# Gate logits from the transposed x on TensorE, or from a second copy of x on VectorE

## The chip, the core and the metric

The kernel runs on one core of a Trainium2 chip. Its engines each work through their own queue in order: TensorE (PE, matrix products; its weight loads are listed as PEld), VectorE (DVE), ScalarE (ACT), GpSimd (POOL) and SyncE (SP, which here only starts DMA transfers). The metric is the device time of one execution in microseconds (us), as the median of several runs.

## The reference

Two attention blocks read the same x of 2048 rows and 1024 columns in bf16, and a gate mixes them row by row. Block A is linear attention over 32 heads of width 32, block B looks at 8 earlier positions, two apart.

```python
x = A_x
g = _sigmoid((x * gate_w).sum(-1, keepdims=True))
a = _A_ref(x, A_wqkv, A_wo)     # phi(q) (phi(k)^T v) / (phi(q) sum(phi(k))), then @ wo
b = _B_ref(x, B_wqkv, B_wo)     # softmax over 8 positions, dilation 2, then @ wo
return g * a + (1 - g) * b      # phi(t) = where(t > 0, t + 1, exp(t)) + 1e-6
```

The gate needs one logit for each of the 2048 rows. With l the logit, the result is (exp(l) * a + b) / (1 + exp(l)); the kernel keeps exp(l) in the tile nel and 1 / (1 + exp(l)) in the tile omg, both 128 x 16: a column for each of the 16 tiles of 128 rows.

## The kernel before, in words

x is read as even and odd rows (two parities, 8 tiles of 128 rows each) and lies transposed in xT, so that it can be the operand of every projection. Two row tiles make a pair; there are 8 pairs.

Most products go by a scheme with seven block products in place of eight (class Group). A group multiplies a 2 x 2 block of x with a 2 x 2 block of weights. Its products m1 to m7 are four matmuls of 512 columns each, and accumulate in the PSUM banks X and Y, of which there are two of each, used by groups in turn. ScalarE saves partial results (M1s, U2s, U4s, line 273), VectorE adds them to the other partial results (acc, line 246). Sums of x blocks (xsums, lines 100 to 103) and of weight blocks (sums, lines 131 to 134) are prepared by VectorE. run (line 427) writes the order of PE by hand: m1 and m2 of the new group, m3 of the one before, m6, m4 of the one before, m7, m5. A bank of Y is thus written by m2, read by VectorE, written again by m7 of the same group, read, added to by m4, read, and then given to the group after the next.

The queues of PE and SP have exactly the order in which the program issues their instructions. The other engines' order is made by a scheduler that keeps dependences and goes by priority. After every product, side (line 384) counts one step on, takes at most one of the deferred VectorE tasks (dve_side, line 405) and, when its turn has come, one step of side work. defer(n, ops, gap) puts a list of VectorE tasks n products ahead; each is placed behind the last accumulation that has been issued (issue_after). later(n, f) calls f n products on. The first due list of deferred tasks goes first; the others wait for the next product.

The stages, in the time of the profile: values of block B (vb_plain and vb_group, lines 505 to 546) to about 70 us, mixed from 48 us on with keys and queries of B (k_group, q_group); then, to about 290 us, a round of four groups that returns every 29.4 us: keys of A for a pair (ka_group), keys of B, values of A (va_group) and queries of B. In that round the attention of B runs as side work: scores into s (line 702, one tile of four PSUM banks, also used for kps, o and oA), their exponentials PT on ScalarE (line 707), masked by VectorE (line 708), the products o with vw (lines 718 and 723), nB and oB on VectorE (lines 730, 734, 736) and a store to OB_d (line 738). The kps matmuls (line 585) take the keys' features eA (phi, line 549: an Exp on ScalarE and three VectorE tasks, lines 552 to 554) and the values vA of a pair. From 290 us follow the queries of A (qa_plain, qa_group, qa_out) and the output projection (out_group).

The gate logits before: gate(t) issues 8 matmuls, one for each 128 of the 1024 columns, with a 128 x 128 tile of xT as weights and one column of gw as the moving operand, into one column of gps (line 456). vb_plain calls it for the first four tiles, the main program for the others, before the groups of pairs 2 to 5. gate_end (line 459) makes nel and omg with two Exp on ScalarE and two VectorE operations. gw is loaded by POOL (line 181). nel is first read by POOL at line 631, in qa_out; omg scales the output groups.

## Time and profile before

| What | us |
|---|---|
| median of 3 runs | 460.13 (459.77 to 460.38) |
| the profiled execution | 459.77 |
| its span | 458.0 |
| TensorE busy in it | 442.6 |
| VectorE busy in it | 283.3 |
| ScalarE busy in it | 237.2 |
| GpSimd busy in it | 60.1 |

The span begins with the first instruction of the profile and ends with the last; what lies around it belongs to the run's time. A row of a timeline or of a chain gives the start, the length, the engine, the source line and the operation with the tile that it writes and the tiles that it reads. The lengths of successive operations of one engine overlap a little, so that the distance from start to start is shorter than the length. Where a row ends in square brackets, they hold the engine's idle time before it and what ended it. In a row of a window the numbers are its time, then the busy time of PE, PEld, DVE, ACT and POOL with their instruction counts, the granted clock of TensorE as a share of full speed (1.00 throughout this profile), the busy share of the DMA engines and what they moved in GB/s.

### The profile page before, as it was taken

To read this page: it belongs to the slowest core of one execution; us is meant where nothing else is said; L and a number is where in the kernel's file an instruction comes from. 1 tells how busy PE (TensorE), PEld (TensorE's weight loads), DVE (VectorE), ACT (ScalarE), POOL (GpSimd) and SP (SyncE) were. 2 spreads that over 40 slices of the span, in tenths; PEclk is the share of its full clock that TensorE was granted. 3 is DMA by queue.
4 is the path that set the end of the run, shared out by engine and by line. 5 is a ranking of instruction groups with operands and counts; after the bars stand their busy time and mean duration, and the time that the engine had idled before them with its cause. 6 is when DMAs were issued, how large, how long until landed. Compare 5 with 4: busy or idle time off the path is not lost.

```text
span 458.0 us, 11713 instructions
## 1 busy us (share of the span) xinstructions
PE 442.6 (97%) x5017; PEld 216.6 (47%) x5070; DVE 283.3 (62%) x452; ACT 237.2 (52%) x345; POOL 60.1 (13%) x119
## 2 busy tenths in 40 slices
PE   8999999998999999999999999999999999999996
PEld 5454444444444444444444444445554444444444
DVE  0566668679657486484774846669777982256112
ACT  3233457467476474673846838536676544222221
POOL 8100000000000000000000000008686314000000
PEclk9999999999999999999999999999999999999999
DMA  8899801880302603007030076291229772795111
GB/s 213 194 203 269 277 2 72 239 158 26 76 4 61 132 3 99 1 27 165 5 99 3 24 156 192 77 253 47 71 79 217 164 173 92 155 204 135 48 46 47
DMA packets 111956, 51.62 MB, mean 113 GB/s; under 512 B 75552, under 2 KB 107552, under 8 KB 111904
## 3 DMA queue, kind: packets, MB, share of 16 engines
q1 hardware_dynamic: 111600, 50.61, 45.9%
q8 instruction: 39, 0.64, 0.6%
q10 hardware_dynamic: 272, 0.26, 0.2%
q14 instruction: 13, 0.11, 0.1%
q0 software_dynamic: 32, 0.00, 0.0%
HBM read 26.22 MB, written 16.78 MB: 94 GB/s over the span
## 4 chain that ended last, share of the span: by engine, by line
PE 90%; ACT 7%; issue 1%; DVE 0%; ACTq 0%; DVEq 0%
PE X L264 41%; PE Y L264 28%; PE Q L667 9%; PE K L520 3%; ACT PT L707 3%; PE o L718 2%; PE oA L624 2%; ACT eA L551 2%; PE s L702 1%; PE kps L585 1%; ACT tA L244 1%; PE o L723 1%; PE Y L299 1%; ACT U2s L273 1%; PE gps L467 1%
## 5 line engine op out<-in xcount | busy, mean ns | idle before, releaser
L264 PEld LDWEIGHTS <-xT 128*128 128x128 bf16 (+1 forms) x352 | 33.0, 98 | 39.6 <-issue 1.8
L264 PE MATMUL X<-T,SS 128*128 128x512 f16 x176 | 45.3, 380 | 0.7 <-ACT U2s L273 0.7
L264 PEld LDWEIGHTS <-WS 128*128 128x128 bf16 (+1 forms) x288 | 28.1, 98 | 33.6
L667 PE MATMUL Q<-xT,WS 128*128 128x512 bf16 x186 | 43.1, 379 | 0.3
L264 PE MATMUL X<-SS,TS 128*128 128x512 f16 x144 | 37.0, 379 | 4.0 <-ACT U2s L273 3.9
L273 ACT COPY U4s<-X 128x512 f32<-128x512 f32 x40 | 23.4, 585 | 33.2 <-PE X L264 33.1
L486 POOL MEMSET vA<- 128x32 bf16 x16 | 4.0, 250 | 268.0 <-DVE eA L554 144.8
L264 PE MATMUL Y<-W,xT 128*128 128x512 bf16 (+1 forms) x152 | 39.0, 379 | 0.0
L264 PEld LDWEIGHTS <-SS 128*128 128x128 f16 x264 | 24.3, 98 | 29.7 <-issue 2.8
L707 ACT ACTIVATE PT<-s 128x2048 bf16<-128x2048 f32 x16 | 29.9, 1870 | 15.1 <-PE s L702 15.0
L264 PE MATMUL Y<-xT,WS 128*128 128x512 bf16 (+1 forms) x144 | 37.0, 379 | 0.0
L264 PEld LDWEIGHTS <-TS 128*128 128x128 f16 x216 | 20.5, 98 | 29.0 <-issue 5.9
L708 DVE TENSOR_TENSOR PT<-PT,maskp 128x2048 bf16<-128x2048 bf16 x16 | 19.6, 1224 | 22.1 <-ACT PT L707 22.1
L273 ACT COPY M1s<-X 128x512 f32<-128x512 f32 x40 | 23.6, 591 | 11.5 <-PE X L264 10.4
L667 PEld LDWEIGHTS <-WS 128*128 128x128 bf16 x192 | 18.3, 98 | 20.1
L273 ACT COPY U2s<-X 128x512 f32<-128x512 f32 x40 | 23.4, 584 | 8.2 <-PE X L264 8.2
L264 PEld LDWEIGHTS <-oT 128*128 128x128 bf16 (+1 forms) x176 | 17.1, 98 | 20.8 <-DMA oT<-OA_d 0.5
L635 POOL TENSOR_TENSOR obA<-ofv,rec 128x512 bf16<-128x512 f32 x22 | 25.6, 1184 | 0.9
L730 DVE COPY nB<-o 128x1024 f32<-128x1024 f32 x16 | 19.5, 1222 | 6.2 <-ACT rB L729 6.2
L729 ACT ACTIVATE rB<-o 128x1024 f32<-128x1024 f32 x16 | 16.4, 1025 | 12.4 <-DVE oB L736 8.2
L264 PE MATMUL X<-T,oS 128*128 128x512 f16 x96 | 22.7, 379 | 0.0
L264 PE MATMUL X<-W,SS 128*128 128x512 bf16 x86 | 22.5, 379 | 0.1
(140 smaller groups left out, 760.1 us busy)
## 6 DMA issues: line engine op xcount, KB each, us to landing
V_d<-va SPq DMA_DIRECT2D x16, 256.0 KB, 3.2
WS<-in_B_wqkv_dram SPq DMA_DIRECT2D x16, 256.0 KB, 4.2
W<-in_A_wqkv_dram SPq DMA_DIRECT2D x8, 512.0 KB, 5.9
vw<-V_d SPq DMA_DIRECT2D x16, 256.0 KB, 4.4
OB_d<-oB SPq DMA_DIRECT2D x16, 256.0 KB, 2.2
OA_d<-obA SPq DMA_DIRECT2D x16, 256.0 KB, 2.3
out_dram<-osb SPq DMA_DIRECT2D x30, 128.0 KB, 1.8
oT<-OB_d SPq DMA_DIRECT2D x12, 256.0 KB, 4.0
```

Of the source, the lines that this page charges most:

```text
L264: nc.tensor.matmul(ps[:], lhsT=lhsT, rhs=rhs, start=start and kc == 0, stop=kc == self.nk - 1, skip_group_check=True)
L273: nc.scalar.copy(out=s[:], in_=ps[:])
L520: nc.tensor.matmul(ps[:], lhsT=xT[p][:, kc, i, c * P:c * P + P], rhs=wvB.W[:, kc, 512 * j:512 * j + 512], start=kc == 0, stop=kc == 7, ski ...
L551: return [lambda: (nc.scalar.activation(out=e, in_=t, func=ACT.Exp), nc.vector.tensor_scalar(out=t, in0=t, scalar1=0.0, scalar2=None, op0= ...
L624: nc.tensor.matmul(o[:, k, 132 * j:132 * j + 132], lhsT=es[i][:, j, k * P:(k + 1) * P], rhs=KVz[:, nn + 4 * j, :], start=True, stop=True)
L635: nc.gpsimd.tensor_tensor(out=ob[:, k:k + 2], in0=of[:, k:k + 2, :, 0:32], in1=rec[:, k:k + 2].broadcast_to([P, 2, 8, 32]), op=ALU.mult)
L667: nc.tensor.matmul(ps[:], lhsT=w.W[:, kc, j * P:j * P + P], rhs=xT[p][:, kc, i, :], start=kc == 0, stop=kc == 7, skip_group_check=True)
L707: nc.scalar.activation(out=PT[:], in_=s[:], func=ACT.Exp, scale=SCALE)
L708: nc.vector.tensor_tensor(out=PT[:], in0=PT[:], in1=maskp[:, None, :].broadcast_to([P, 4, 512]), op=ALU.mult)
L718: nc.tensor.matmul(o[32 * g:32 * g + 32, 2 * b, cols], lhsT=vw[rows, j, 4 * ch + g, :], rhs=PT[rows, g, cols], start=True, stop=True)
L729: nc.scalar.activation(out=rB[:], in_=o[:, 1:4:2, :], func=ACT.Ln)
L730: nc.vector.tensor_copy(out=nB[:], in_=o[:, 0:4:2, :])
```

## The change

The gate matmuls, gw's load by POOL and all calls of gate in the early stage are taken out. From the stage of B's keys and queries on, gates() loads the gate row into the first half of a new tile gx, in all 128 partitions alike, and 44 products later calls gate(0). gate(t) loads the 128 rows of tile t, as they are in x, into the second half of gx. Four products later VectorE gets two tasks, one product apart: each multiplies 512 columns with the gate row, in place, and puts the sums over the columns into logit. With the second task the next tile's gate is called, so its load is issued then; it overwrites the same half of gx. After tile 15, gate_end adds the two halves and makes nel (one Exp) and omg from nel. gx has the buffer that is later used by the tile of of qa_out; an assertion there says that nel has been issued.

In the lists of the other engines the following moves: some of the VectorE tasks of phi come a product later, because the pieces have taken their turn, and one of x's sums comes earlier in the first stage. PE keeps its order apart from the matmuls that are left out.

```diff
-    gw = consts.tile([P, 8], BF16, name="gw")
-    nc.gpsimd.dma_start(out=gw[:], in_=gate_w.rearrange("(k p) -> p k", p=P))
...
-    gps = gps_tile[:, 0, 0:16]
+    gx = ofp.tile([P, 2, D], BF16, name="gx", tag="of", bufs=1)
+    logit = consts.tile([P, 2, 16], F32, name="logit")
 
     def gate(t):
-        p, j = divmod(t, 8)
-        hf, c = divmod(j, 4)
-        for kc in range(8):
-            nc.tensor.matmul(gps[:, t:t + 1], lhsT=xT[p][:, kc, hf, c * P:(c + 1) * P], rhs=gw[:, kc:kc + 1],
-                             start=kc == 0, stop=kc == 7)
+        gw, xg = gx[:, 0, :], gx[:, 1, :]
+        nc.sync.dma_start(out=xg, in_=xrows(t))
+
+        def part(h):
+            cols = slice(512 * h, 512 * h + 512)
+            nc.vector.scalar_tensor_tensor(out=xg[:, cols], in0=xg[:, cols], scalar=1.0, in1=gw[:, cols],
+                                           op0=ALU.mult, op1=ALU.mult, accum_out=logit[:, h, t:t + 1])
+            if h:
+                gate(t + 1) if t < 15 else gate_end()
+        defer(4, [lambda: part(0), lambda: part(1)])
 
     def gate_end():
-        nc.scalar.activation(out=nel[:], in_=gps, func=ACT.Exp)
-        nc.scalar.activation(out=omg[:], in_=gps, func=ACT.Exp)
-        nc.vector.tensor_scalar(out=omg[:], in0=omg[:], scalar1=1.0, scalar2=None, op0=ALU.add)
+        ready.add("nel")
+        nc.vector.tensor_tensor(out=nel[:], in0=logit[:, 0, :], in1=logit[:, 1, :], op=ALU.add)
+        nc.scalar.activation(out=nel[:], in_=nel[:], func=ACT.Exp)
+        nc.vector.tensor_scalar(out=omg[:], in0=nel[:], scalar1=1.0, scalar2=None, op0=ALU.add)
         nc.vector.reciprocal(out=omg[:], in_=omg[:])
+
+    def gates():
+        nc.sync.dma_start(out=gx[:, 0, :], in_=bass.AP(gate_w.tensor, gate_w.offset, [[0, P], [1, D]]))
+        later(44, lambda: gate(0))
...
-            gate(tile_of(*t))
             v_final(vs[t[0]], True)(t[1], 0, ps[t][:], None)
...
+            assert "nel" in ready
...
-    gates(2)
...
-    later(2, lambda: gates(3))
...
-    gates(4, 5)
...
-    gates(6, 7)
-    gate_end()
...
+    gates()
     run(lambda: vb_group(6), RATE_R)
```

## The prediction

> **What bounds the kernel now.** I read the page first: TensorE is busy in nearly every slice, VectorE is not.

> ```profile
> PE 442.6 (97%) x5017; PEld 216.6 (47%) x5070; DVE 283.3 (62%) x452; ACT 237.2 (52%) x345; POOL 60.1 (13%) x119
> PE   8999999998999999999999999999999999999996
> DVE  0566668679657486484774846669777982256112
> ```

> So a microsecond taken from TensorE (PE) is a microsecond of time, and work on VectorE (DVE) is free as long as PE never waits for it. Next, the chain that ended last, in order of time, and the view of line 456, the gate matmuls that go:

> ```profile
> 32.70 0.78 PE gps L456 x32
> 39.55 0.78 PE gps L456 x32
> ...
> L456 PE MATMUL gps<-gw,xT x128: 163/163/167, 10.0 to 40.2; 128*128 128x1 bf16 x128
> ```

> All gate work lies on that chain before 41 us: 32 matmuls push the next product back by 0.78 us, 24 ns each; the 163 ns of one overlap. Then the stretch in which the new VectorE work falls, as a window (time, PE, PEld, DVE, ACT, POOL, clock, DMA), and its timeline at the places where PE follows VectorE closely:

> ```profile
> 112.70:207.00 94.30, 91.35 (x1457) 44.16 (x1469) 63.63 (x102) 59.82 (x78) 1.68 (x7) 1.00 0.22 54
> ...
> 118.91 0.69 DVE L246 TENSOR_TENSOR qT<-Y,M1s 128x512 bf16<-128x512 f32 x1
> 119.75 1.03 PE L264 MATMUL Y<-xT,WS 128*128 128x512 f16 x4
> 119.95 0.69 DVE L246 TENSOR_TENSOR vA<-Y,U2s 128x512 bf16<-128x512 f32 x1 [0.36 <-PE Y L264]
> 121.57 0.68 PE L585 MATMUL kps<-vA,eA 128*32 128x33 bf16 x64
> ...
> 139.14 1.22 DVE L730 COPY nB<-o 128x1024 f32<-128x1024 f32 x1
> 140.41 0.74 PE L718 MATMUL o<-PT,vw 64*32 64x57 bf16 x72
> ...
> 156.08 0.69 DVE L246 TENSOR_TENSOR qT<-Y,U2s 128x512 bf16<-128x512 f32 x1 [1.54 <-PE Y L264]
> 156.84 0.77 PE L702 MATMUL s<-qT,kT 32*64 32x57 bf16 x72
> ```

> The reader is to see four thin slacks, from VectorE's end to the PE start that depends on it: qT from M1s frees the Y bank of the next product, 0.15 us; vA from U2s is read by the kps matmuls, 0.93; the copy nB frees o for the second o matmuls, 0.05; qT from U2s is read by the scores, 0.07. The places recur every 29.4 us; the slack of the first varies from 0.15 to 1.6, the last two stay under 0.4. Last, prices of loads and of the nearest VectorE operation:

> ```profile
> OB_d<-oB SPq DMA_DIRECT2D x16, 256.0 KB, 2.2
> xr<-in_A_x_dram SPq DMA_DIRECT2D x2, 256.0 KB, 3.6
> out_dram<-osb SPq DMA_DIRECT2D x4, 64.0 KB, 1.6
> ...
> 299.69 1.28 DVE L677 SCALAR_TENSOR_TENSOR eq<-Q,eq 128x512 bf16<-128x512 f32 x2
> ```

> **What is removed.** 128 gate matmuls with their weight loads. The chain's pieces add to 0.38+0.18+0.18+0.38+0.38+0.78+0.78 = 3.1 us. This shortens the time in full: PE's longest idle before 42 us that is not start-up is 0.5 us behind a ScalarE copy, and that copy moves up with PE. The transposed x loads are the nearest cover to fail: SP issues them 1.5 us apart from 22.76, so those of pair 4 (the first two, 5.7 us to landing) are in by 30; the group that reads them moves from 33.3 to 31.0. Also gone are POOL's gate load (1.04 us, on an engine busy 13% of the span), one Exp of 0.18 on ScalarE, and two small VectorE operations moved to about 207: nothing. POOL now clears maskp (0.54) ahead of ident's select; the transposes wait for xr, landing 3.9, and ident is ready near 2: nothing.

> **What is added.** One broadcast load of the gate row, 60 us before use: nothing. Sixteen loads of 256 KB on SP and 32 pieces on VectorE; a piece is a 512-column scalar_tensor_tensor with an accumulator output. The pieces of tile t must finish before SP may load tile t+1 into the same buffer, and the program issues the first piece of t+1 four products later. By the changed program's instruction order, tile 0's pieces stand before the copy nB at 114.10 and tile 15's after L736 at 204.93.

> *Price of a piece:* two L677 take 1.28, one 0.68, so one follows the other by 0.60. For the accumulator I add 0.06, half the 0.12 between the tiny VectorE operation at 41.14 and its successor. Ends: 0.33 (the pace of the 512-column 16-bit sums, 33.97 to 34.30) and 0.92 (the slower scalar_tensor_tensor of L855, 0.75, with a whole tiny operation of 0.17). I take 0.66, as L677 is the same operation and width.

> *Price of a load:* stores of 64 and 256 KB land after 1.6 and 2.2, 0.003 us per KB; the quickest vw load lands after 2.1, taken as one of 32 KB; 224 KB more make 2.8. Ends: 2.0 (quickest OB_d store) and 4.1 (slower xr load, among other loads). I take 2.8.

> *What it does.* 32 x 0.66 = 21 us fit the 30.7 us that VectorE idles in the stretch. But VectorE works in order: a first piece whose load hasn't landed stops every accumulation queued behind it. I walked the changed order through this profile's times, before's clock throughout, each operation at its start-to-start pace; D is how far PE has fallen back.
> - Tile 0 and the exponentials' operations that the pieces push behind them: qT from M1s ends at 120.24 and the product due at 119.75 starts at 120.3: 0.55. Tile 1's load stands on SP behind both OB_d stores, whose second waits for L736 (117.4): issued 117.75, landed 120.55. Its pieces run 120.75 to 122.07, ahead of vA from U2s, so kps, due 122.12, starts 122.8: 0.7. D 1.25.
> - Tile 3's second piece ends 133.86, tile 4's load lands 136.7, VectorE stands idle for it 1.6 us; the work behind makes nB end at 142.87, and the second o matmuls, due 141.66, start 142.95: 1.3. D 2.55.
> - Tile 6 puts tA from M1s to 158.64, product due 158.43: 0.3. Its second piece ends 156.92, tile 7's load lands 159.75, both pieces stand ahead of qT from U2s, which ends 161.76; scores due 159.64: 2.2. D 5.0.
> - Tiles 8 to 10, same way: qT from M1s 0.8. D 5.85.
> - Tile 12's first piece waits for its load until 192.05; scores due 192.08, start 193.45: 1.4. D 7.2.
> - Tiles 14 and 15: nB 0.2, the product on Y before vA's U4s is read 0.3. D 7.7.

> ScalarE's new nel waits for tile 15 ahead of the copies vA and U2s; U2s ends at 216.1, its reader is due at 216.5: nothing. nel is first used by POOL's rec near 300. SP's queue: the WS load of 154.35 now stands behind tile 8's load until 161.1, its sums stood at 165.87 and D moves them to 170.9: nothing. vw is delayed by 2 to 3 us, read 17 us later: nothing. Should those covers go, the price is the delay itself.

> Sum: 7.7 - 3.1 = +4.6 us. The profiled execution took 459.77 us (span 458.0 and 1.77 around it), the median of the three runs is 460.13, 0.36 above; so 464.4 by the profile and **464.7** as a median. With both prices at their low ends D is about 0.6 (net -2.5, 457.6), with both high about 20 (net +17, 477).

> [...]

> **Rivals.**
> - *The cover holds (faster).* VectorE has the idle time, and four products of 0.86 us, 3.5 us, lie between a tile's last piece and the next one's first. If pieces take 0.42 and loads 2.2, the walk leaves D at about 1.9: net -1.2, 458.9. It decides where D passes 3.1: with loads at 2.2 that is a piece of about 0.55. Against it: the tiles' pieces stand directly ahead of qT from U2s, and L677's pace.
> - *Loads are slow here.* WS loads in this stretch took 4.6 (146.80 to the sums at 151.44) and share the queue. At 4.1 and 0.66 each of four waits grows by 1.3, and two more (tile 2's, tile 11's) by about 1: D 15, net +12, 472.
> - *The gates cost nothing where they were* (the start bound by loads): the 3.1 is not gained, 467.8. Against: PE stands in the chain throughout.
> - *Mere occupancy:* the loads hide and only the pieces push: of the terms 0.55, 0.7, 0.3, 0.8, 0.2 and 0.3 stay, 2.9, against 3.1: 459.9.

> **How the numbers follow.** Forecast (+1 to +9) 0.60; slow loads or a dear accumulator (over +9) 0.10; gates free 0.03; mere occupancy, within 0.2% (0.92 us, about what this kernel's measurement can tell) 0.10; cover holds 0.17. Slower is 0.73. The range leaves out a tenth below and a tenth above: 458.9, the cover case, to 471, near the slow loads. The forecast's own range is 461 to 469.

> **What would show it.** Before 41 us: no L456, and everything after it about 3.1 us early until 112. Then in 112 to 220: 32 pieces near 0.7 each, VectorE waiting for gx loads ahead of qT from U2s, PE waits at scores, kps and o put down to VectorE, DVE busy over 85%. After about 220 the two profiles should run in step, some 4.6 us apart. Wrong if gx loads land within about 2.2 us or pieces take 0.4: then PE shows no new waits.

## The result, and the profile after

The changed kernel takes 464.93 us (median, 464.78 to 467.14), the kernel before 460.10 beside it (459.77 to 460.38): a ratio of 1.0116, with a 95% interval of 1.0085 to 1.0147. It is slower by 4.8 us; the forecast was 464.7. The profiled execution took 465.0, its span is 463.2 against 458.0.

From the page of the changed kernel: busy times, then busy tenths of PE and DVE and the granted clock in 40 slices of 11.6 us.

```profile
PE 441.7 (95%) x4890; PEld 213.5 (46%) x4942; DVE 302.1 (65%) x517; ACT 236.8 (51%) x344; POOL 59.0 (13%) x118
...
PE   8999999999988899999999999999999999999996
...
DVE  0576777679678698697683755759777883256112
...
PEclk9999999999998999999999999999999999999999
```

PE is busy for 0.9 us less in a longer span: the three 8s, from 127 to 162 us, are new. One slice, from 139 us, also has a lower clock; the kernel before has a 9 in all forty.

The view of the tile gx (durations in ns: least, median, most; then idle time by what ended it; then the loads' trip):

```profile
L457 DVE SCALAR_TENSOR_TENSOR gx<-gx x32: 680/686/694, 110.1 to 210.7; 128x512 bf16<-128x512 bf16 x32
L457 DVE DVE_READ_ACCUMULATOR gx<-gx x32: 80/83/89, 110.7 to 211.3; 128x1 f32 x32
...
  DMA gx<-in_A_x_dram: 10.3, 5
...
DMA to landing us min/median/max: 2.6/2.8/6.1
```

VectorE stood idle 10.3 us in five waits for these loads. The chain of waits around the most expensive one, followed back from 145 us (start, us, what):

```profile
124.81 2.80 DMA gx<-in_A_x_dram
...
127.70 0.70 DVE gx L457 x2
...
130.14 0.62 DVE gx L457 x2
...
130.78 3.38 DMA gx<-in_A_x_dram
...
134.25 0.70 DVE gx L457 x2
134.95 0.60 DVE tA L244
135.55 1.13 DVE PT L717
136.68 0.61 DVE gx L457 x2
...
139.17 1.15 DVE nB L739
140.31 0.04 issue
140.35 0.74 PE o L727 x72
```

In this view, `DVE gx L457 x2` is one piece with the read of its accumulator. So the rows are tile 3's load, its two pieces, tile 4's load, its first piece, two operations that stand between in VectorE's order, its second piece, and behind that everything up to the copy nB, which the second o matmuls wait for. The waits of PE (us, times, longest) name all places of the forecast but that of tile 6:

```profile
PE o L727 <- DVE nB L739: 2.8, 3, 2.0
PE s L711 <- DVE qT L244: 2.3, 2, 1.3
...
PE Y L262 <- DVE qT L244: 0.7, 2, 0.5
...
PE kps L593 <- DVE vA L244: 0.4, 1, 0.4
```

And the clock, in windows around the wait for nB (time, PE busy, clock, DMA share, GB/s):

```profile
137.59:141.00 3.41, 1.39 (x84) 1.00 0.22 77
141.00:144.41 3.41, 3.19 (x26) 0.50 0.21 82
```

For 3.41 us from 141.00 PE runs at half clock. The table lists by how much each place pushed PE back, from the starts of the same matmuls in the two profiles; the changed kernel comes to 110 us with a lead of 2.95.

| place (start before, after) | forecast | measured |
|---|---|---|
| product behind qT, tile 0 (119.75, 117.19) | 0.55 | 0.40 |
| product behind kps, tile 1 (122.18, 120.07) | 0.7 | 0.45 |
| second o matmuls, tile 4 (140.41, 140.35) | 1.3 | 2.06 |
| half clock (143.08, 144.66) | none | 1.64 |
| tA from M1s, tile 6 | 0.3 | 0 |
| product behind the scores, tile 7 (157.53, 160.46) | 2.2 | 1.35 |
| tiles 8 to 10 (178.52, 182.11) | 0.8 | 0.67 |
| scores, tile 12 (186.93, 191.60) | 1.4 | 1.08 |
| tiles 14, 15 (207.08, 212.09) | 0.5 | 0.34 |
| D | 7.7 | 7.99 |

The distance between the profiles is 5.0 us from there on (score matmuls start at 274.48 and 279.49), and with the lead of 2.95 that makes 7.96; the rows add to 7.99 because each is rounded.

### The profile page after: what moved, and what is told of

Read it like the earlier page. It is cut to its first block, busy times and chain, and to the rows that moved or that the text cites. A ratio compares the mean times of both kernels' runs of the same rounds, so it can differ in the third digit from the quotient of the medians.

```text
span 463.2 us, 11566 instructions
## 1 busy us (share of the span) xinstructions
PE 441.7 (95%) x4890; PEld 213.5 (46%) x4942; DVE 302.1 (65%) x517; ACT 236.8 (51%) x344; POOL 59.0 (13%) x118
## 4 chain that ended last, share of the span: by engine, by line
PE 74%; DVE 9%; ACT 6%; DMA 5%; issue 2%; SPq 2%; DVEq 0%; ACTq 0%
PE X L262 33%; PE Y L262 23%; PE Q L676 9%; DMA gx<-in_A_x_dram 4%; PE K L529 3%; DVE gx L457 3%; ACT PT L716 2%; PE o L727 2%; PE oA L633 1%; DVE nB L739 1%; ACT eA L559 1%; SPq L816 1%; DMA oT<-OA_d 1%; PE s L711 1%; ACT tA L242 1%
## 5 line engine op out<-in xcount | busy, mean ns | idle before, releaser
L262 PEld LDWEIGHTS <-xT 128*128 128x128 bf16 (+1 forms) x352 | 33.3, 98 | 40.7 <-issue 2.6
L457 DVE SCALAR_TENSOR_TENSOR gx<-gx 128x512 bf16<-128x512 bf16 x32 | 21.2, 687 | 10.4 <-DMA gx<-in_A_x_dram 10.3
## 6 DMA issues: line engine op xcount, KB each, us to landing
V_d<-va SPq DMA_DIRECT2D x16, 256.0 KB, 3.3
WS<-in_B_wqkv_dram SPq DMA_DIRECT2D x16, 256.0 KB, 4.8
vw<-V_d SPq DMA_DIRECT2D x16, 256.0 KB, 5.1
OB_d<-oB SPq DMA_DIRECT2D x16, 256.0 KB, 2.2
gx<-in_A_x_dram SPq DMA_DIRECT2D x16, 256.0 KB, 2.8
OA_d<-obA SPq DMA_DIRECT2D x16, 256.0 KB, 2.3
```

Source lines behind the costliest of these rows:

```text
L262: nc.tensor.matmul(ps[:], lhsT=lhsT, rhs=rhs, start=start and kc == 0, stop=kc == self.nk - 1, skip_group_check=True)
L457: nc.vector.scalar_tensor_tensor(out=xg[:, cols], in0=xg[:, cols], scalar=1.0, in1=gw[:, cols], op0=ALU.mult, op1=ALU.mult, accum_out=logi ...
```

## The experiments

The theory: a piece costs little; what costs is that the next load is issued only when the second piece has read the buffer, so that its trip stands in VectorE's order ahead of accumulations that PE waits for. Rivals: the pieces' own 20 us on an engine that is nearly the bound, and, for the half clock, a cause other than the wait. D is always PE's place against the kernel's own place before 110 us, measured at the score, o and kps matmuls.

### No pieces at all

```diff
 def gates():
-    nc.sync.dma_start(out=gx[:, 0, :], in_=bass.AP(gate_w.tensor, gate_w.offset, [[0, P], [1, D]]))
-    later(44, lambda: gate(0))
+    nc.vector.memset(logit[:], 0.0)
+    later(44, gate_end)
```

> The changed kernel without the sixteen x loads, the gate row load and the 32 pieces: logit is cleared once, so the gate is 1/2 everywhere and the logits are not computed. It measures what taking the gate matmuls off TensorE is worth by itself. Theory (the gates stood on the chain, 3.0 us of it): about 457.1 us, 3.0 under the kernel before. Rival (the early stage is bound by loads and the gates cost nothing there): 460.1.

Measured: 456.51 us (455.96 to 459.04) against 459.59 for the kernel before; ratio 0.9942, interval 0.9921 to 0.9962. The gate matmuls were worth 3.1 us, as on the chain before, and nothing in the changed order without pieces costs anything: the distance between the two profiles stays the same within 0.02 us from 97 to 274 us. All that the changed kernel loses, it loses by loads and pieces. This run also shows where VectorE idles in a round; its timeline (start, duration; in brackets the idle time ahead of the instruction and what ended it):

```profile
117.71 0.69 DVE L244 TENSOR_TENSOR vA<-Y,U2s 128x512 bf16<-128x512 f32 x1 [0.36 <-PE Y L262]
120.06 0.69 DVE L244 TENSOR_TENSOR qT<-Y,U4s 128x512 bf16<-128x512 f32 x1 [1.65 <-ACT U4s L271]
120.66 0.42 DVE L598 COPY KVacc<-kps 128x264 f32<-128x264 f32 x1
121.95 0.69 DVE L244 TENSOR_TENSOR tA<-Y,M1s 128x512 bf16<-128x512 f32 x1 [0.86 <-PE Y L262]
124.47 0.69 DVE L244 TENSOR_TENSOR qT<-Y,U2s 128x512 bf16<-128x512 f32 x1 [1.83 <-PE Y L262]
127.97 1.23 DVE L717 TENSOR_TENSOR PT<-PT,maskp 128x2048 bf16<-128x2048 bf16 x1 [2.81 <-ACT PT L716]
```

Four gaps of 1.65, 0.86, 1.83 and 2.81 us stand in one corner of the round; the rest of it has shorter ones, 0.90 and 1.17 us the longest.

### One load instead of sixteen

```diff
-    nc.sync.dma_start(out=xg, in_=xrows(t))
+    if t == 0:
+        nc.sync.dma_start(out=xg, in_=xrows(t))
```

> All 32 pieces stay in their places, but x is loaded only for tile 0, so no piece of a later tile waits for a load (the logits of tiles 1 to 15 are not those of their rows). It separates the waits for loads from the pieces' mere occupancy of VectorE. Theory (two thirds of the delay come from VectorE standing before a load that hasn't landed): PE falls back about 2.4 us in the stretch in place of 8.0, no clock dip, about 459.5 us. Rival (the pieces' 20 us on VectorE are the cost, whether the loads are late or not): 464 to 465.

Measured: 459.16 us (458.11 to 460.84), ratio 0.9991 (0.9979 to 1.0003). D is 1.69, less than the 2.4 of the theory, and VectorE waits for no load. With the 32 pieces in the same list of deferred tasks and no trips, PE loses 1.7 us in place of 8.0: the trips carry the other 6.3, the half clock among them (5.8 by the medians, 464.93 - 459.16).

### The trip halved and moved forward

```diff
+def load_x(t, h):
+    nc.sync.dma_start(out=gx[:, 1, 512 * h:512 * h + 512], in_=xrows(t)[:, 512 * h:512 * h + 512])
 ...
-    nc.sync.dma_start(out=xg, in_=xrows(t))
 ...
     def part(h):
         ...
+        if t < 15:
+            load_x(t + 1, h)
```

> Each tile of x is loaded in two halves of 512 columns; the half of the next tile is issued as soon as the piece that read the same half is done, a product earlier for the first half and with 128 KB in place of 256. Theory (a load's trip against the time between the pieces decides): each wait ahead of a first piece shrinks by 1.2 to 1.5 us, the second o matmuls wait under 1 us and the clock doesn't dip, scores lose 0.3 and 0.2 in place of 1.35 and 1.1: about 460.3 us. Rival (occupancy): 464 to 465. If the queue of SP is the limit, its 15 more issues of 0.33 us make it slower than 464.9.

Measured: 461.42 us (461.06 to 461.74), ratio 1.0041 (1.0026 to 1.0056). D is 4.07 where about 3.2 was expected (460.3 less the 457.1 put down for the run without pieces), most of the 1.1 us over the expected time. Idle time for loads falls from 10.3 in five waits to 4.9 in four (trips 2.1/2.4/6.1), and the wait for nB is gone; at tile 7's place more is left than I expected. The timeline of PE in this run:

```profile
155.61 0.33 PE L715 MATMUL s<-qT,kT 32*64 32x57 bf16 x32
157.97 0.50 PE L715 MATMUL s<-qT,kT 32*64 32x57 bf16 x40 [2.03 <-DVE qT L244]
```

Two pieces still stand ahead of qT from U2s, the first with a load's wait of 1.40 us. PE waits 2.03 us here, as long as for nB in the changed kernel, and the clock stays at 1.00.

### Tile 4's pieces two products later

```diff
-    defer(4, [lambda: part(0), lambda: part(1)])
+    defer({4: 6, 5: 2}.get(t, 4), [lambda: part(0), lambda: part(1)])
```

> Only tile 4's pieces are put two products later and tile 5's delay is shortened by two, so that from tile 5 on all pieces stand where they stood. The first piece of tile 4 then stands behind the masking of PT and no longer holds up nB. Theory (TensorE's clock dips because it stood idle 2.0 us at that place): the 2.0 us wait and the 1.6 us of slow matmuls behind it both go, about 461.3 us, granted clock 1.00 throughout. Rival (the dip is due to something else in that stretch): only the wait goes, 462.9, and a dip stays near 142.

Measured: 463.29 us (462.92 to 464.59), ratio 1.0087 (1.0072 to 1.0103). Without the wait there is no half clock either, in windows as above:

```profile
137.60:141.00 3.40, 3.37 (x93) 1.00 0.24 82
141.00:144.40 3.40, 3.40 (x17) 1.00 0.20 77
```

At the place itself 3.67 us are gone (D just before tile 7 falls from 4.53 to 0.86). At tile 7 the scores now wait 1.91 us in place of 1.28 and a product 0.23 on tA, and 1.0 comes back there; D ends at 5.35 against 7.96 by the same matmuls, 2.6 less. The time falls by less: by 2.1 between the profiled executions (462.92 and 465.0), because this one is already 0.6 us later before 110 us, and by 1.6 between the medians. So in the profiled execution the half clock belongs to that wait, but what a deferred piece avoids at one place it partly pays at the next, which my 461.3 had left out. Of the four executions, the slowest (464.59) has a mean clock of 0.995, as the changed kernel has with its one fall; where it fell, no profile of it shows.

### All pieces in the gaps, five behind three accumulations

Each half has its own load, issued behind the piece that last read it, and the pieces are called where the accumulation is issued, with no deferral:

```diff
+def piece(count):
+    for _ in range(count):
+        ...
+        with tc.issue_after(last_dve[0]):
+            last_dve[0] = nc.vector.scalar_tensor_tensor(...).ins
+        if n + 2 < 32:
+            load_x(n + 2)
 ...
 # va_group, final:
+    if (i, j) == (1, 0):
+        piece(1)
 # ka_group, final:
+    if (i, j) == (0, 0):
+        piece(1)
 # q_group, final:
+    if (i, j) == (1, 0):
+        piece(3)
```

> All 32 row-product pieces are computed, so this is the whole work of the changed kernel, but their places and loads differ: each half of x has its own load, issued behind the piece that last read its half buffer, and the pieces stand behind operations after which VectorE was idle in the run without pieces: one behind vA <- Y,U2s (idle 1.65 to 1.77 us there), one behind tA <- Y,M1s (1.80 us), three behind qT <- Y,U2s (2.81 us), in six rounds, and two more. Theory (pieces and loads cost only what the product or softmax behind them waits for): the third piece behind qT needs a load issued one piece earlier, 2.4 us, and ends about 0.8 us behind the time at which PT could start; PT has some room, so 456.5 plus 6 x 0.3 = 458.3 (457.3 to 459.5), below the kernel before. Rival (23 us of more VectorE work cost time wherever they stand, since VectorE is the second bound of this stage): 461 to 462, as the run with half loads.

Measured: 460.76 us (458.19 to 462.72), ratio 1.0014 (0.9991 to 1.0038): above the theory's range, and for the most part not by the pieces. Up to 280 us PE falls back by 0.46 us in all, although VectorE waits longer for loads than in the changed kernel (14.4 us in seven waits), mostly at the third piece behind qT. The rest comes at one place, in the middle of a group of o matmuls, where PE pauses and the profile shows nothing that it waits for:

```profile
285.99 0.66 PE L747 MATMUL o<-PT,vw 64*32 64x57 bf16 x62 [0.39 <-DVE nB L759]
289.16 0.23 PE L747 MATMUL o<-PT,vw 64*32 64x57 bf16 x10 [2.51 <-issue]
```

Behind the 2.51 us stands half a clock for 3.4 us (another 1.7). In the run without pieces the same pause, ahead of the same ten matmuls, is 0.68 us with no half clock. D, the later start of these o matmuls behind nB, the difference in the pause and the half clock, 0.46 + 0.36 + 1.83 + 1.7, make the 4.3 us between the two profiled executions (461.76 and 457.43). All ten executions have the same pieces, yet six of them have a mean clock of 0.996 and took 460.3 to 462.7, while the four at 0.999 or 1.000 took 458.2 to 459.4, inside the theory's range.

### The same with one piece moved, to give its load more time

```diff
 # kv, behind KVacc:
+    piece(1)
 ...
 # q_group, final:
-        piece(3)
+        piece(2)
```

> As the run with five pieces in the gaps, but one of the three pieces behind qT <- Y,U2s stands behind KVacc instead (idle 0.86 us there), so that every piece finds its half already landed (over 3 us between a load's issue and its use, against 2.4 us of trip). Theory: no load ends a wait and no piece is longer than its gap except in the rounds where weight sums fill the place behind KVacc: 457.0 (456.5 to 458.0), 2.5 us under the kernel before and 8 under the changed one. Rival (the VectorE work itself costs): 461 to 462.

Measured: 458.22 us (457.94 to 461.22), ratio 0.9982 (0.9965 to 1.0000). VectorE's timeline in the corner of the round shown above (of the rows left out in it, those of 0.08 us are the reads of the accumulator):

```profile
120.03 0.42 DVE L612 COPY KVacc<-kps 128x264 f32<-128x264 f32 x1
120.37 0.68 DVE L467 SCALAR_TENSOR_TENSOR gx<-gx 128x512 bf16<-128x512 bf16 x1
...
121.32 0.69 DVE L244 TENSOR_TENSOR tA<-Y,M1s 128x512 bf16<-128x512 f32 x1 [0.26 <-PE Y L262]
121.93 0.68 DVE L467 SCALAR_TENSOR_TENSOR gx<-gx 128x512 bf16<-128x512 bf16 x1
...
123.84 0.69 DVE L244 TENSOR_TENSOR qT<-Y,U2s 128x512 bf16<-128x512 f32 x1 [1.22 <-PE Y L262]
124.45 0.68 DVE L467 SCALAR_TENSOR_TENSOR gx<-gx 128x512 bf16<-128x512 bf16 x1
...
125.06 0.69 DVE L467 SCALAR_TENSOR_TENSOR gx<-gx 128x512 bf16<-128x512 bf16 x1
...
127.34 1.23 DVE L738 TENSOR_TENSOR PT<-PT,maskp 128x2048 bf16<-128x2048 bf16 x1 [1.59 <-ACT PT L737]
```

The accumulations start where they did: the rows that both runs have lie 0.63 us earlier here than in the run without pieces, and PE is ahead by the same 0.63 us before any piece. The pieces have only filled the idle time. Up to 280 us, 30 pieces push PE back by 0.14 us. That is the clearest answer to the rival: the 20 us of VectorE work cost next to nothing. The theory expected every load in time. In fact VectorE waited for loads in five places, 4.3 us in all, but only one wait (0.35 us, at 153 us) stands where the 0.14 was lost, ahead of a qT. The time is not the 457.0 of the theory because of what comes after 280 us. In the profiled execution (460.29) the pause is 1.67 us, with 1.7 us of half clock behind it. Six of the ten executions took 457.9 to 458.3, at a mean clock of 0.998 to 1.000.

### Long waits for nB in the kernel before: how the clock falls

```diff
-    nc.vector.tensor_copy(out=nB[:], in_=o[:, 0:4:2, :])
+    for _ in range(3 if ch == 0 else 1):
+        nc.vector.tensor_copy(out=nB[:], in_=o[:, 0:4:2, :])
```

> The kernel before, with the copy nB of the first o of each softmax (eight places) made three times instead of once, so that TensorE waits for it by 2 x 1.13 us more: about 2.0 to 2.8 us at each place. Theory (the clock falls to a half for 3.4 us where a wait of about 2 us fills enough of a window that runs free of the kernel's work): the dip comes at some of the eight places and not at others; 459.6 + 8 x 2.1 = 476 without dips, 1.6 us more for each dip, so 478 to 487. Rival (length alone decides, with a threshold of about 2.0 us): a dip at all eight, 489. Rival (the dip of the changed kernel has nothing to do with the wait): none, 476.

Measured: 496.1 us (one execution, beside a median of 459.6). The eight waits were 2.67, 3.78, 2.96, 3.14, 2.96, 3.14, 2.96 and 3.03 us, longer than I had put them; together they are 24.6. The clock fell behind seven of them, not behind the first. Windows of 3.41 us, laid where the clock changes:

```profile
74.95:78.36 3.41, 1.41 (x7) 1.00 0.00 0
78.36:81.77 3.41, 2.74 (x89) 1.00 0.17 63
112.49:115.91 3.42, 1.27 (x6) 1.00 0.00 0
115.91:119.32 3.41, 1.78 (x82) 0.50 0.00 0
119.32:122.73 3.41, 3.41 (x10) 0.50 0.20 77
150.04:153.45 3.41, 1.34 (x82) 1.00 0.02 5
153.45:156.87 3.42, 3.42 (x9) 0.50 0.21 77
```

The first wait, 76.36 to 79.03, is cut by a border of this grid into 2.00 and 0.67: full clock. The second and third leave their windows busy for 1.27 and 1.34 us: half clock in the next one. Behind the second it lasts two windows; the wait ran on into the first of them, which was busy for 1.78 us. The seven falls start at 115.905, 153.452, 187.585, 221.718, 255.852, 289.985 and 324.118, which is 0, 11, 21, 31, 41, 51 and 61 times 3.4133 us from the first. They come between 1.64 us before the end of the wait and 1.34 us after it. So these rows agree with the theory of a window that runs free of the kernel's work, and not with a threshold by the wait's length: the wait of 2.67 us had no fall behind it, the 2.02 of the changed kernel had one. The time adds up: 24.6 of waits less the 0.6 that the kernel before has, and eight windows at half clock, seven for 1.7 each and the one of 1.78 us busy for half of that, 0.9, make 459.6 + 24.0 + 12.8 = 496.4.

With three copies more:

> The same with the copy made four times: 3 x 1.13 us more, waits of 3.1 to 3.9 us. Theory (share of a free window): a dip at nearly all eight places, 459.6 + 8 x 3.2 + 7 x 1.6 = 496. Rival (threshold by length, about 2.0 us): the same here. Rival (no bond between wait and clock): no dip, 485.

Measured: 508.9 us (one execution). All eight waits (3.9 to 5.3 us) were followed by a fall, three of them by one of two windows; the starts lie 0, 12, 22, 33, 43, 54, 64 and 75 times 3.4133 us from the first. The first two readings expected a fall at all eight places or nearly so; this run decides only against the third, no bond between wait and clock. It was sized too low again, since the waits were longer.

### Pieces begun earlier, so that none is left in the last round

```diff
-    later(44, lambda: (load_x(0), load_x(1), pieces.update(on=True)))
+    later(10, lambda: (load_x(0), load_x(1), pieces.update(on=True)))
 ...
-    piece(1)                       # va_group
+    piece(1 if pair % 2 else 2)
```

> As the run with gaps and no wait, all pieces computed, but they begin some 45 us earlier (the first loads ten products behind the gates' start) and two stand behind vA <- Y,U2s in every second round, so that the 32nd is done in the fifth round, near 245 us, and no load of x stands on the queue ahead of A_wo's weights. In the run before, 30 pieces moved TensorE by 0.14 us against the run without pieces up to 276 us, and its time came from a pause of 1.67 us without a wait inside the o matmuls at 285.8 us, a chunk of code late behind 2.3 MB of transfers, with a stretch at half clock behind it. Theory (the pause comes with the sixth round's loads, which push A_wo's weights later): no pause, 456.8 (456.3 to 457.5), 2.8 us under the kernel before. Rival (the pause comes from where the code chunks lie against those weights, whatever the loads of x do): 458.2 to 460.3, as the run before.

Measured: 460.31 us (458.35 to 461.90), ratio 1.0009 (0.9994 to 1.0024): at the upper end of the rival's range, but not for the rival's reason. The pause shrank to 0.63 us in the profiled execution, as the theory had it, but PE lost time at three other places: 1.51 us by the early pieces (o waits 1.68 us for nB), 0.33 at the weight sums near 158 us, and 1.11 where gate_end now came in ScalarE's order ahead of a softmax exponential. ScalarE's timeline there:

```profile
246.00 0.22 ACT L478 ACTIVATE nel<-nel 128x16 f32<-128x16 f32 x1 [2.95 <-DVE nel L477]
246.12 1.86 ACT L737 ACTIVATE PT<-s 128x2048 bf16<-128x2048 f32 x1
```

A 0.22 us exponential that waits for the last piece holds back PT, and PT holds back ScalarE's U4s, which PE needs.

### Begun at the old place, gate_end held back

```diff
-    later(10, lambda: (load_x(0), load_x(1), pieces.update(on=True)))
+    later(44, lambda: (load_x(0), load_x(1), pieces.update(on=True)))
 ...
-    later(2, gate_end)
+    later(9, gate_end)             # its operations under tc.issue_after(last_dve[0])
```

> All pieces computed. As the run done by 250, but begun at the old place again (first pieces near 117 us), and the sum, exponential and reciprocal of the gates held back by nine products, so that ScalarE does not wait in them for the last piece ahead of a softmax exponential. In the run done by 250 TensorE fell back by 1.51 us at the early pieces (o waits 1.68 us for nB at 109.7), 0.33 at the weight sums near 158 and 1.11 where the gates' exponential waited 2.95 us on ScalarE ahead of PT; its pause in the o matmuls was 0.63 us, as without pieces (0.68). Theory (these three and nothing else made its time): the first and the last go, the two loads of the sixth round are issued early in it and leave the pause at 0.6 to 0.7: 457.0 (456.5 to 457.8), 2.7 us under the kernel before. Rival (the sixth round's loads bring the pause back, as in the run with gaps and no wait): 458.2 to 460.3.

Measured: 457.54 us (457.44 to 459.06) against 459.63; ratio 0.9955, interval 0.9941 to 0.9969. It computes everything and beats the kernel before by 2.1 us and the changed one by 7.4. Its page and the view of gx:

```profile
PE 440.2 (96%) x4890; PEld 213.2 (47%) x4942; DVE 302.9 (66%) x517; ACT 236.6 (52%) x344; POOL 58.8 (13%) x118
```

```profile
L467 DVE SCALAR_TENSOR_TENSOR gx<-gx x32: 678/685/693, 118.0 to 272.6; 128x512 bf16<-128x512 bf16 x32
...
  DMA gx<-in_A_x_dram: 9.5, 11
```

VectorE does as much as in the changed kernel (302.9 against 302.1 us) and waits for loads nearly as long (9.5 against 10.3), but D is 0.57 when all 32 pieces are done: all but one of the waits lie in time in which VectorE had nothing due. The one loss is 0.56 at the scores near 155 us, where a piece behind the weight sums waits 1.01 us for its load ahead of qT. The gates' sum and reciprocal, now at 282 to 284 us, stand ahead of nB and cost another 0.23. The pause in the o matmuls was 1.34 us in the profiled execution (459.06, the slowest of five), not the 0.6 to 0.7 that I expected, so its cause stays open.

## Why the prediction was right, and where it was not

**The removal.** -3.1 was read off the chain: the run without pieces gives 456.51 - 459.59 = -3.08. The rival that the gates cost nothing falls.

**Prices.** The load was put at 2.8 from the nearest stores and loads; the median is 2.8, the least of the sixteen 2.6, and the five that ended VectorE's waits took 3.66, 2.80, 3.38, 2.78 and 2.62, 3.05 in the mean. The 4.6 that I gave as the time of WS loads runs from the first of two issues to the sums; the two loads took 3.27 and 4.11. The piece was put at 0.66 and is 0.61 to 0.62 from start to start (110.08, 110.69, 111.31). The accumulator's output is an instruction of its own here, the row of 80 to 89 ns above; the pace with it is only about 0.01 over the 0.60 of L677 without, where I had taken 0.06.

**The terms.** Of the eight places forecast seven show a loss, and the total of 7.7 against 7.99 looks better than it is. Two terms were too small. The o matmuls at tile 4 were put at 1.3 and cost 2.06: the trip there was 3.38, not 2.8, and the two terms before it had come out 0.40 smaller, so that PE was due earlier. The half clock behind that wait, 1.64, was not in the sum at all. The others are together 2.2 smaller than forecast (4.3 against 6.5). Of the 0.85 at tile 7, part lies in how PE starts: 32 of the 72 score matmuls ran at 158.42, ahead of the rest at 160.03, where I had all of them wait for qT; part in PE that was later already by the half clock, and so waited less (D ahead of this place was 4.53, in the forecast 2.85). Tile 6's 0.3 vanished for that reason too, as far as the profile shows; I have no run on it alone. The prediction kept "before's clock throughout", and so put the half clock at nothing without a reason; errors of +0.8 and +1.6 against -2.2 nearly cancel. The mechanism was well read, but that the sum came so close was luck.

**Nothing-terms.** SP's queue, the WS and vw loads behind the gx loads, nel on ScalarE: the distance of 5.0 us does not change from 212 to 279 us, so they cost nothing, as written. The run done by 250 shows that nel's cover was a matter of place: 1.11 us when it was issued ahead of PT.

**The signs to look for.** VectorE over 85% busy between 112 and 220 us was wrong: it was 84.52 of 108.0 us, 78%. The sign was too high from its own terms: the 63.6 us of before and 21 of pieces in 94.3 + 7.7 us make 83%, and less once the window reaches 220 us, beyond the last piece. The rest came as written: 32 pieces near 0.7, waits at o, scores, kps and the product on Y, and the two profiles in step at the end.

**The rivals.** Mere occupancy is what the run with one load makes real: 459.16, with D at 1.69 where the rival had 2.9. It did not happen because the trips were not hidden. Loads were not slow throughout: the median is the 2.8 put down, though three of the sixteen took 3.8 to 6.1. The cover held in the versions with the pieces in the gaps, not in this one: there the same 20 us cost 0.14 to 0.57. So "VectorE has 30.7 us idle" was true and also beside the point; where in the order the pieces and the waits for their loads stand decided.

## What to carry to other kernels

In these runs the idle time of an engine that works in order was cover only for work that stood directly ahead of the wait that makes the idle time: the same 32 pieces cost 8.0 us as deferred tasks with their loads, 1.7 as deferred tasks without them, and 0.6, loads included, behind the accumulations after which VectorE had to wait anyway. A load that reuses a single buffer put its whole trip, 2.8 us in the median, into that order; halves loaded one use ahead cut the waits for it from 10.3 us to 4.9, and what is left (9.5 us of waits in the last run) can be put where nothing is due. And before a wait of TensorE is priced, look at what comes behind it: here one of 2 us cost another 1.6 by the clock.

## What the runs showed of the hardware that was not expected

The other finding is the pause of PE with nothing that the profile shows to wait for, ahead of the last 8 or 10 of 72 o matmuls. It stands in ten of the twelve profiles, the kernel before (0.82 us) and the changed one (0.54) among them, and lasts 0.54 to 2.51 us. In all ten PE goes on 2.37 to 2.59 us after the start of a 16 KB packet on a DMA queue that the profile calls instruction (the chunk of code of the expectations above). The later that packet starts against the o matmuls, the longer the pause: 1.30 us ahead of the first of them in the changed kernel, 0.80 us after it in the run with five pieces. In the two kernels with extra copies it starts 4.5 and 5.7 us ahead of them, and there is no pause. So in these twelve profiles the pause goes with that packet; that the one makes the other is not shown. Why the packet comes when it does stays open: the four loads of A_wo's weights, 2.1 MB, are on the DMA engines at the time, but that they hold it up is argued, not shown.
